# A gated mix of linear attention and a GLU: the gate's transposition, M's loads, the parts of kv and the first forms

## The chip, the cores and the metric

The kernel runs on one core of one Trainium2 chip. The time is that of one execution on the device in microseconds (us), taken as the median of several runs. Beside the runs there is one profiled execution, whose rows are quoted below. The core has five engines that work from queues of their own: TensorE (PE: matrix products into PSUM), VectorE (DVE), ScalarE (ACT), GpSimd (POOL) and SyncE (SP). SyncE and GpSimd issue the transfers here, each in the order of its own queue.

## The reference

x has 2048 rows (tokens) of 640 columns. The result is `g * a + (1 - g) * b` with three parts:

```python
g = _sigmoid((x * gate_w).sum(-1, keepdims=True))

q, k, v = qkv[0], qkv[1], qkv[2]            # 32 heads of 20 columns
phi = lambda t: jnp.where(t > 0, t + 1, jnp.exp(t)) + 1e-6
pq, pk = phi(q), phi(k)
kv = jnp.einsum("bhsd,bhse->bhde", pk, v)
z = jnp.einsum("bhsd->bhd", pk)
num = jnp.einsum("bhqd,bhde->bhqe", pq, kv)
den = jnp.einsum("bhqd,bhd->bhq", pq, z)[..., None] + 1e-6
a = (num / den) @ wo                        # heads side by side

h = _sigmoid(x @ w_gate) * (x @ w_up)       # 1536 columns
b = h @ w_down
```

All inputs are float32. The gate g is one number per token.

## The kernel before

Every product is made in float32r from two halves of each operand: a high half (the operand rounded) and a low half (the operand less its high half). `mm3` (L215 to L218) issues three matmuls, high by high, low by high and high by low. So each operand needs a "form": ScalarE copies the high half, and VectorE subtracts it for the low half (`split`). Most of the larger products are arranged by a scheme of seven products instead of eight (`Block`, steps s1 to s7), with sums of quarters on VectorE. The tile names `ch`, `dd`, `cc` and `rot` are the four kinds of PSUM tile, two buffers each; `tb` holds the sum of b in SBUF.

The order of the instructions on all engines is fixed when the program is built. The class `Order` keeps an estimate of the time of TensorE, ScalarE and VectorE. Work that isn't needed at once is queued with its cost on ScalarE and VectorE, a key and a time from which it is ready; `order.fill()` issues what fits behind TensorE's account, and `order.need(key)` forces what has that key. A few instructions more or less in the account therefore shift the places of others.

The stages, in the profile's time:

- 0 to about 140 us: k = x @ wk and phi(k), and Gt = x' @ phi(k), gathered in `gt`. The columns of `wk` carry the gate's weights too, so that a product's last column is the gate's logit; `vec_copy` puts it into `logit` (one column per tile of 128 tokens, 16 in all). The loop over `k` at the beginning (L747 on) makes forms of the first 128 columns of x and of `wk` as they arrive: `plain_a` (forms `xah`, `xal` of x), `k_plain` (`k1h`, `k1l` and, in the tiles named `pkh` and `pkl`, the second half of `wk`), `plain_b12` (`b12h`, `b12l`).
- about 145 to 190 us: q for half of the tokens (`q_phase(1)`), in 13 steps. In between, `kv_part(hg)` makes kv for six heads at a time from `wv` and `gt` (L1240), takes its diagonal blocks with the mask `bd` (`kvt`) and makes its forms `kvh` and `kvl`; `m_part(hg)` multiplies by that part of `wo` (`woh`, `wol`), copies the product to `ms` and stores it into `m_dram`. M is kv and wo multiplied together, 640x640. With six heads a part there are five parts of 120 columns and one of 40. `order.follow` puts `kvl` behind `kvh`, and `m_part` calls `order.need(("kv", hg))`.
- about 190 to 400 us: `f_phase(1)`, twelve blocks (f = 0 to 11) of the GLU's hidden columns for the second half of the tokens: products with `wg`, `wu` and `ws` (the forms of the gate's, the up's and the summed weights), sigmoid, product, forms `hf`, and the product with `wd`. The forms of weights are also stored, to be read again. In block 1, after step 4, stands `gate_store` (L1113): TensorE multiplies `logit` with an identity matrix in `gs`, which turns 128x16 into 16x128; ScalarE makes sigmoid(l) and sigmoid(-l); SyncE stores both into `gate_dram` and then copies the first, repeated for each head, into `gate_rep`. `gs` is made on VectorE from an iota of GpSimd.
- about 400 to 460 us: q for the first half of the tokens; about 460 to 665 us: `f_phase(0)`, the same twelve blocks for that half. The stored forms are loaded two blocks ahead: in the loop, block f + 2 loads `wg` after step 2, `wu` after step 6 and `ws` after step 7 of block f. In odd blocks from 3 on the products with `wd` are made in pairs by the seven-product scheme (`down_pair`), with a tile `wf` that `load_wf` loads in three pieces. Beside it `queue_m` loads M's rows, makes their forms and stores them into `mp_dram` (key "m", the lowest in rank), and `queue_den` makes the denominators of the attention for a group of 512 tokens: sums on VectorE into `fac`, a store to `den_dram`, four loads that turn it, a reciprocal times the gate, a store to `fac_dram` and four loads back.
- about 665 us to the end: the result's columns from M, phi(q) and the factors, added to b times (1 - g).

For the last stage two kinds of M's pieces are loaded in `f_phase(0)` at block 11 (FC - 1): `load_m(0)` gets forms from `mp_dram`, and `load_ms(0)` and `load_ms(1)` get M's raw columns by `m_rows`: four transfers for each of four column groups, sixteen in all, on GpSimd's queue, into `mt`, `mr` and `mv`. Ahead of them a loop forces what is left with the key "m".

Of the kernel before, what the change touches and what calls it, by code (L numbers as in the profile page):

```python
# [6 lines left out]

F32 = mybir.dt.float32
F32R = mybir.dt.float32r
I32 = mybir.dt.int32  # L10
AF = mybir.ActivationFunctionType
OP = mybir.AluOpType
PSUM = bass.MemoryType.PSUM
# [2 lines left out]
P = 128  # L16
# [7 lines left out]
HW = HALF + 2  # L24
CW = 256
HPG = 6
NHG = -(-H // HPG)
EPS = 1e-6


# [158 lines left out]
def v_cost(w):  # L189
    return 0.155 + w * 0.00104  # L190
# [3 lines left out]
def gated_mix_kernel(ctx: ExitStack, tc: tile.TileContext, xt, xn, wk, wv, wo, wst_q, wst_f, out_t):  # L194
# [17 lines left out]
    def ps_tile(tag):  # L212
        return psum.tile([P, 512], F32, name=tag, tag=tag, bufs=2)
# [47 lines left out]
    bd = common.tile([HPG * DH, HPG, DH], F32, name="bd")  # L261
    zcol = common.tile([P, KC], F32, name="zcol")
    zeps = common.tile([P, 1], F32, name="zeps")
    logit = common.tile([P, S // P], F32, name="logit")
    gs = common.tile([P, P], F32, name="gs")
    fac = common.tile([P, NG, TG], F32, name="fac")
    p_dram = dram.tile([P, KC, NG, TG], F32, name="p_dram")
# [448 lines left out]
    class GTBatch:  # L716
# [18 lines left out]
        def out(self, u):  # L735
# [6 lines left out]
            else:  # L742
                add(dst, ps, dst, "p")


    c0 = chunks[0]
    order.pe = 8.0  # L747
    b0, b1 = KPlain(0), KPlain(1)
    for k in range(KC):
        order.act = max(order.act, order.pe - 1.5)  # L750
        c0.plain_a(k, k + 1)
        k_plain(k)
        if k < 2:
            c0.plain_b12(k, k + 1)
        else:
            c0.plain_b(k, k + 1)
        order.pe = max(order.pe, order.vec)
        b0.k(k)
        if k < 2:
            b1.k(k)  # L760
        if k == 1:
            load_xn(0)
            load_xn(1)
# [10 lines left out]
            split_xn(1)  # L774


    ij = fac[:, 0, :P].bitcast(I32)
    nc.gpsimd.iota(ij, pattern=[[1, P]], base=P, channel_multiplier=-1)
    nc.gpsimd.memset(ones_f, 1.0)
    nc.gpsimd.affine_select(bd, ones_f[:bdn, :bdn].rearrange("p (b c) -> p b c", c=DH),  # L780
                            pattern=[[-DH, HPG], [0, DH]], base=0, channel_multiplier=1,
# [20 lines left out]
    for c in range(1, 4):  # L802
        ck = chunks[c]
        if c == 1:
            a, b = KPlain(2), KPlain(3)
            order.need((ck, "plain"))
            queue_ks()
            queue_xn(2)
            for k in range(KC):
                a.k(k)  # L810
                order.fill()
            a.phi_a()
            for k in range(KC):
                b.k(k)
                order.fill()
                if k == 0:
                    a.phi_b()
                    order.add(0, 0.25, lambda: vec1(gs, ij, float(P), op0=OP.is_equal))
                    queue_qw(2)
            order.need(("ks", 5))  # L820
            for t in range(2):
                k_split(tok(2, t))
        else:
            a, b = KBlock(2 * c), KBlock(2 * c + 1)
            for n in range(1, 6):
                order.need((ck, n))
                if c == 2 and n >= 3:
                    order.need(("ks", (1, 0, 2)[n - 3]))
                getattr(a, f"s{n}")()
                getattr(b, f"s{n}")()  # L830
            order.need((ck, 6))
            if c == 2:
                order.need(("ks", 5))
            if c + 1 < len(chunks):
                chunks[c + 1].load()
            else:
                nx = [Chunk(1, i, None, i * CW, xst_v, (b12h, b12l)) for i in range(2)]
                nx[0].load()
            queue_xn(2 * c)
            a.s6()  # L840
            a.s7()
            a.sum_b()
            a.phi_a()
            b.s6()
            a.phi_b()
            order.need(("pk", 2 * c - 1))
            k_split(tok(2 * c, 0))
            b.s7()
            b.sum_b()
            k_split(tok(2 * c, 1))  # L850
        if c == 3:
            pa_cm.__exit__(None, None, None)
            px_cm = tc.tile_pool(name="px", bufs=1, side="right", reuse_waits="tile")
            px = px_cm.__enter__()
            xf = XForms(px, TG)
            pg_cm = tc.tile_pool(name="pg", bufs=1, side="right", reuse_waits="tile")
            pg = pg_cm.__enter__()
            W, WT = {}, {}

            def wg_tile():  # L860
                return pg.tile([P, 2, D], F32R, name="wg", tag="wg", bufs=2)

            def put(n, i, t):
                WT[n, i] = t
                W[n, i] = [t[:, c] for c in range(2)]

            def store_w(n, i):

                key = n[::2] + (i,)
                w_dram[key] = dram.tile(list(WT[n, i].shape), F32, name="w%s%d%d" % key)  # L870
                nc.gpsimd.dma_start(w_dram[key], f32(WT[n, i]))

            def wg_split(n, src):
                put(n, 0, wg_tile())
                split(*W[n, 0], src)
                if n[0] == "f":
                    order.then(lambda: store_w(n, 0))
            nx[0].f = nx[1].f = xf
        elif c == 1:
            chunks[2].load(lag=6.0)  # L880
        g = GTBatch(c, batches[c])
        order.need(("xn", 2 * c))
        if c < 3:
            chunks[c + 1].queue()
        else:
            queue_xn(7)
        for u in range(4):
            g.part(u, 0, 2, ("rot", "dd", "ch", "cc")[u])
            if u == 0:
                b.phi_a()  # L890
            if u == 1:
                b.phi_b()
        queue_split(2 * c + 1)
        if c < 3:
            queue_xn(2 * c + 1)
        else:
            w_stage = [m1_tile("ma", "w0") for _ in range(2)]
            for n in range(2):
                nc.sync.dma_start(w_stage[n], wst_q[:, n])
            queue_forms(nx)  # L900
        for u in range(2 * KC):
            g.part(u, 2 if u < 4 else 0, 4)
            order.fill()
# [23 lines left out]
    def tt(name, dt=F32, shape=(P, TG)):  # L927
        return pw.tile(list(shape), dt, name=name, tag="t", bufs=4)
# [184 lines left out]
    def gate_store():  # L1113

        n = S // P
        ps = ps_tile("rot")[:n, :P]
        nc.tensor.matmul(ps, logit, gs, start=True, stop=True)
        order.on_pe(4, P)
        t = tt("gates")[:n, :2 * P]
        for i in range(2):  # L1120
            act(t[:, i * P:(i + 1) * P], ps, AF.Sigmoid, "p", scale=1.0 - 2 * i)
        for i in range(2):
            nc.sync.dma_start(gate_dram[i].rearrange("(i p) -> i p", p=P), t[:, i * P:(i + 1) * P])
        nc.sync.dma_start(gate_rep, gate_dram[0].rearrange("(i o p) -> i o p", o=1, p=P).broadcast_to([n, H, P]))

    def queue_den(g, place=None):
# [59 lines left out]
    MV, MO, MO_AT, ZP = {}, {}, {}, []  # L1186

    def hg_slice(hg):
        c0 = hg * bdn
        return c0, min(bdn, D - c0)  # L1190

    def load_mv(hg):
        if hg < NHG:
# [41 lines left out]
    def kv_part(hg, tag="ch"):  # L1235
        c0, w = hg_slice(hg)
        v = MV[hg]
        ps = ps_tile(tag)
        for m in range(KC):
            nc.tensor.matmul(ps[:w, :w], v[:, m, :w], gt[:, m, c0:c0 + w], start=(m == 0), stop=(m == KC - 1))  # L1240
        order.on_pe(10, 2 * bdn)
        kvt = mp.tile([bdn, bdn], F32, name="kvt", tag="kvt", bufs=2)
        vec2(kvt[:w, :w], ps[:w, :w], bd.rearrange("p b c -> p (b c)")[:w, :w], OP.mult, "p")
        kvh = mp.tile([bdn, bdn], F32R, name="kvh", tag="kvh", bufs=3)
        kvl = mp.tile([bdn, bdn], F32R, name="kvl", tag="kvl", bufs=3)
        act(kvh[:w, :w], kvt[:w, :w], AF.Copy, "v")
        KV[hg] = (kvh, kvl)
        order.follow(v_cost(bdn), lambda: vec2(kvl[:w, :w], kvt[:w, :w], f32(kvh[:w, :w]), OP.subtract), ("kv", hg))
        load_mv(hg + 3)

    def m_part(hg, tag="cc"):
        c0, w = hg_slice(hg)
        order.need(("kv", hg))
        order.need(("wo", hg))
        (kvh, kvl), (woh, wol) = KV.pop(hg), WO.pop(hg)
        ms = m1_tile(("ma", "mb")[hg % 2], "ms", F32, bdn)
        for h in range(2):
            ps = ps_tile(tag)
            cs = slice(h * HALF, (h + 1) * HALF)
            mm3(ps[:w, :HALF], kvh[:w, :w], kvl[:w, :w], woh[:w, cs], wol[:w, cs], True, True)  # L1260
            act(ms[:w, cs], ps[:w, :HALF], AF.Copy, "p")
        nc.gpsimd.dma_start(m_dram[c0:c0 + w], ms[:w])
        queue_wo(hg + 2)
# [435 lines left out]
    def f_phase(pr, q, hooks={}):  # L1699
# [51 lines left out]
        for f in range(FC):  # L1751
# [1 line left out]
                order.need(("h", f // 2 - 1, "T3"), False)  # L1753
            down = iter(())
            if not pr and f % 2 and f > 1:
                if f == FC - 1:
                    while any(it[3] == "m" for it in order.spare) or order.pend:
                        order.need("m")
                        order._flush()
                    load_m(0)  # L1760
                    load_ms(0)
                    load_ms(1)
                down = down_pair(f // 2 - 1)
            for s in (3, 4, 5):
                step(f, s)
# [86 lines left out]
    def load_forms(kind, f, *forms):  # L1852
# [1 line left out]
            load_form((kind, 0, f), i)  # L1854

    tail = f_phase(1, q, {
        (1, 4): [gate_store],
        (9, 4): [load_x2],
        (FC - 2, 7): [lambda: load_forms("q", 2, 1, 2)],
        (FC - 1, 2): [lambda: load_forms("q", 2, 0), lambda: queue_a(0, 2), lambda: queue_a(2, 4)],  # L1860
# [402 lines left out]
```

## Time and profile before

| | us |
|---|---|
| runs of before: median (lowest to highest of 3) | 744.03 (742.05 to 745.65) |
| the profiled execution's own time | 745.79 |
| its span, first to last instruction | 744.1 |

The span is the time between the first and the last instruction that the profile shows; what lies around it is the rest of 745.79. In rows of a timeline the columns are: start in us from the span's start, length in us, engine, line, operation, tile written and tiles read, size, count, and in brackets how long the engine had stood idle and what ended that. "SPq" and "POOL DMA_DIRECT2D" rows are issues of transfers; their landing is another row (KB each, us from issue to landing). A matmul's row is longer than its pitch, because matmuls overlap: the distance from start to start is what counts. PEld is the load of the stationary operand.

### The profile page before, as it was taken

How to read it: one execution, taken by the hardware profiler on the slowest of the kernel's cores; microseconds unless marked ns; L12 is line 12 of the kernel's file. 1: busy time of each engine (PE TensorE's matmuls, PEld its weight loads, DVE VectorE, ACT ScalarE, POOL GpSimd, SP SyncE). 2: the span in 40 equal slices, each digit the busy share in tenths (PEclk: the TensorE clock that was granted, in tenths of full speed). 3: DMA queues.
4: the chain of work that ended last, by engine and by line, in shares of the span. 5: the costliest groups of instructions: out<-in, count | busy, mean ns of one | idle time of the engine just before them, and what ended most of it. 6: DMA issues, size and time to landing. Idle time of an engine off the chain costs nothing.

```text
span 744.1 us, 10181 instructions
## 1 busy us (share of the span) xinstructions
PE 736.6 (99%) x3628; PEld 631.4 (85%) x3628; DVE 547.8 (74%) x961; ACT 332.3 (45%) x629; POOL 107.7 (14%) x174
## 2 busy tenths in 40 slices
PE   9999999999999999999999999999999999999998
PEld 7999999987888888888888888888888888788886
DVE  4888676967577778877877964556778777788976
ACT  5664638258555634333434365343323322224541
POOL 0221212012222311312210211000000002200000
PEclk9999999999999999999999999999999999999999
DMA  8564727699888777676966758986869655959312
GB/s 275 121 183 112 197 64 217 177 282 320 295 331 294 264 263 286 220 265 223 370 242 224 297 171 316 359 240 227 278 231 331 253 182 214 274 192 346 116 71 100
DMA packets 69848, 175.23 MB, mean 235 GB/s; under 512 B 11038, under 2 KB 30286, under 8 KB 66213
## 3 DMA queue, kind: packets, MB, share of 16 engines
q1 hardware_dynamic: 52533, 109.46, 45.0%
q0 software_dynamic: 17120, 64.96, 24.8%
q8 instruction: 28, 0.46, 0.3%
q14 instruction: 23, 0.19, 0.1%
q10 hardware_dynamic: 144, 0.16, 0.1%
HBM read 105.65 MB, written 63.91 MB: 228 GB/s over the span
## 4 chain that ended last, share of the span: by engine, by line
PE 88%; DMA 5%; DVE 3%; ACT 2%; SPq 1%; issue 1%; DVEq 0%
PE ch L216 9%; PE ch L217 9%; PE ch L218 9%; PE dd L217 8%; PE dd L216 8%; PE dd L218 8%; PE cc L218 7%; PE cc L216 7%; PE cc L217 7%; PE rot L216 6%; PE rot L217 6%; PE rot L218 6%; DMA xst<-xt 3%; DMA ws<-wf 2%; DMA wo_sb<-wo 1%
## 5 line engine op out<-in xcount | busy, mean ns | idle before, releaser
L228 ACT ACTIVATE c<-ch 128x512 f32<-128x512 f32 x87 | 51.9, 596 | 169.3 <-PE ch L218 167.5
L232 DVE TENSOR_TENSOR hf<-c,hf 128x512 fp32r<-128x512 f32 x63 | 43.3, 689 | 40.4 <-ACT hf L228 40.4
L232 DVE TENSOR_TENSOR c<-cc,c 128x512 f32<-128x512 f32 x54 | 37.2, 689 | 31.9 <-ACT c L228 22.4
L232 DVE TENSOR_TENSOR tb<-dd,tb 128x512 f32<-128x512 f32 x73 | 49.7, 688 | 14.8 <-PE dd L218 14.6
L228 ACT ACTIVATE c<-c 128x512 f32<-128x512 f32 x57 | 35.8, 629 | 49.9 <-DVE c L232 49.6
L228 ACT ACTIVATE hf<-c 128x512 fp32r<-128x512 f32 x63 | 39.2, 624 | 17.4 <-DVE c L232 17.0
L232 DVE TENSOR_TENSOR tb<-rot,tb 128x512 f32<-128x512 f32 (+1 forms) x61 | 40.8, 678 | 6.3 <-PE rot L218 6.1
L216 PE MATMUL ch<-xth,ws 128*128 128x512 f32 x108 | 42.3, 392 | 1.9 <-DMA ws<-wf 1.7
L218 PE MATMUL ch<-xth,ws 128*128 128x512 f32 x108 | 42.0, 389 | 0.0
L217 PE MATMUL ch<-xtl,ws 128*128 128x512 f32 x108 | 42.0, 389 | 0.0
L216 PE MATMUL dd<-xrh,wg 128*128 128x512 f32 x93 | 36.4, 391 | 0.0
L218 PE MATMUL dd<-xrh,wg 128*128 128x512 f32 x93 | 36.2, 389 | 0.0
L217 PE MATMUL dd<-xrl,wg 128*128 128x512 f32 x93 | 36.2, 389 | 0.0
L216 PE MATMUL rot<-pkh,xnh 128*128 128x320 f32 x102 | 31.6, 310 | 0.5 <-DVE gt L232 0.5
L217 PE MATMUL rot<-pkl,xnh 128*128 128x320 f32 x102 | 31.5, 309 | 0.0
L216 PE MATMUL cc<-xbh,ws 128*128 128x512 f32 x81 | 31.5, 389 | 0.0
L217 PE MATMUL cc<-xbl,ws 128*128 128x512 f32 x81 | 31.5, 389 | 0.0
L218 PE MATMUL cc<-xbh,ws 128*128 128x512 f32 x81 | 31.5, 389 | 0.0
L218 PE MATMUL rot<-pkh,xnl 128*128 128x320 f32 x102 | 31.4, 308 | 0.0
L232 DVE TENSOR_TENSOR c<-c,c 128x512 f32<-128x512 f32 x44 | 30.2, 686 | 1.3 <-ACT c L228 0.9
L228 ACT ACTIVATE ws<-wsum 128x512 fp32r<-128x512 f32 (+1 forms) x24 | 16.1, 679 | 22.9 <-DVE wsum L232 22.9
L216 PEld LDWEIGHTS ch<-xth,ws 128*128 128x128 f32 x108 | 20.3, 188 | 6.9 <-issue 2.3
(564 smaller groups left out, 2266.6 us busy)
## 6 DMA issues: line engine op xcount, KB each, us to landing
wf<-ws POOLq DMA_DIRECT2D x12, 1152.0 KB, 6.7
ws<-wf SPq DMA_DIRECT2D x12, 1152.0 KB, 8.4
wst<-wst_f SPq DMA_DIRECT2D x12, 640.0 KB, 4.9
wf<-wg POOLq DMA_DIRECT2D x12, 640.0 KB, 5.2
wd<-wd POOLq DMA_DIRECT2D x12, 640.0 KB, 5.5
wg<-wf SPq DMA_DIRECT2D x12, 640.0 KB, 5.7
xst<-xt SPq DMA_DIRECT2D x10, 640.0 KB, 7.7
wf<-wd SPq DMA_DIRECT2D x10, 640.0 KB, 5.7
```

What stands on the lines that cost most here:

```text
L216: nc.tensor.matmul(out, l_hi, r_hi, start=first, stop=False, skip_group_check=True)
L217: nc.tensor.matmul(out, l_hi, r_lo, start=False, stop=False, skip_group_check=True)
L218: nc.tensor.matmul(out, l_lo, r_hi, start=False, stop=last, skip_group_check=True)
L228: nc.scalar.activation(out, src, fn, **kw)
L232: nc.vector.tensor_tensor(out, a, b, op=op)
```

## The change

Four things are changed.

1. `gate_store` no longer uses TensorE. `logit` gets 32 columns (16 of them zero); ScalarE makes both sigmoids on 128x32; VectorE turns them in blocks of 32x32; SyncE stores them in four transfers (one for each 32 rows) in place of two, and then `gate_rep` as before. The iota, the comparison and `gs`'s identity are gone. The call moves from block 1 to block 2.
2. `load_ms(0)` and `load_ms(1)`, with the loop ahead of them, stand in block 9 (FC - 3) in place of 11; `load_m(0)` stays in 11.
3. kv's heads are cut at 0, 6, 12, 17, 22, 27 and 32: two parts of 120 columns and four of 100. `kvh` is made by VectorE, directly followed by `kvl`; nothing is queued any more.
4. The first pass of the loop at the beginning is written out: VectorE makes `k1h` and `k1l`, ScalarE makes `xah` and the second half's high form.

```diff
-NHG = -(-H // HPG)
+HG = (0, 6, 12, 17, 22, 27, 32)
+NHG = len(HG) - 1
...
-    logit = common.tile([P, S // P], F32, name="logit")
+    logit = common.tile([P, H], F32, name="logit")
...
+    def first_forms():
+
+        x, (xh, xl) = c0.x[0][:, 0:1], c0.f.a_part(0, 1, c0.cs)
+        w1, w3 = wk_st[0][:, lo_h], wk_st[0][:, hi_h]
+        act(xh, x, AF.Copy)
+        vec_copy(k1h[:, 0], w1)
+        vec2(k1l[:, 0], w1, f32(k1h[:, 0]), OP.subtract)
+        vec2(xl, x, f32(xh), OP.subtract, "a")
+        split(k3h[:, 0], k3l[:, 0], w3)
...
-        c0.plain_a(k, k + 1)
-        k_plain(k)
+        if k:
+            c0.plain_a(k, k + 1)
+            k_plain(k)
+        else:
+            first_forms()
...
-    ij = fac[:, 0, :P].bitcast(I32)
-    nc.gpsimd.iota(ij, pattern=[[1, P]], base=P, channel_multiplier=-1)
+    nc.gpsimd.memset(logit[:, S // P:], 0.0)
...
-                    order.add(0, 0.25, lambda: vec1(gs, ij, float(P), op0=OP.is_equal))
...
     def gate_store():
 
         n = S // P
-        ps = ps_tile("rot")[:n, :P]
-        nc.tensor.matmul(ps, logit, gs, start=True, stop=True)
-        order.on_pe(4, P)
-        t = tt("gates")[:n, :2 * P]
+        t = tt("gates").rearrange("p (a n c) -> p a n c", n=2, c=H)
         for i in range(2):
-            act(t[:, i * P:(i + 1) * P], ps, AF.Sigmoid, "p", scale=1.0 - 2 * i)
-        for i in range(2):
-            nc.sync.dma_start(gate_dram[i].rearrange("(i p) -> i p", p=P), t[:, i * P:(i + 1) * P])
+            act(t[:, 0, i], logit, AF.Sigmoid, scale=1.0 - 2 * i)
+        order.on_vec(2 * H, "a")
+        nc.vector.transpose(t[:, 1], t[:, 0])
+        for b in range(P // H):
+            nc.sync.dma_start(gate_dram.rearrange("n (i b c) -> b i n c", b=P // H, c=H)[b],
+                              t[b * H:b * H + n, 1])
...
     def hg_slice(hg):
-        c0 = hg * bdn
-        return c0, min(bdn, D - c0)
+        h0, h1 = HG[hg:hg + 2]
+        return h0 * DH, (h1 - h0) * DH
...
-        act(kvh[:w, :w], kvt[:w, :w], AF.Copy, "v")
+        vec_copy(kvh[:w, :w], kvt[:w, :w])
+        vec2(kvl[:w, :w], kvt[:w, :w], f32(kvh[:w, :w]), OP.subtract)
         KV[hg] = (kvh, kvl)
-        order.follow(v_cost(bdn), lambda: vec2(kvl[:w, :w], kvt[:w, :w], f32(kvh[:w, :w]), OP.subtract), ("kv", hg))
...
-        order.need(("kv", hg))
...
-                if f == FC - 1:
+                if f == FC - 3:
                     while any(it[3] == "m" for it in order.spare) or order.pend:
                         order.need("m")
                         order._flush()
-                    load_m(0)
                     load_ms(0)
                     load_ms(1)
+                elif f == FC - 1:
+                    load_m(0)
...
-        (1, 4): [gate_store],
+        (2, 4): [gate_store],
```

More of the change, by code (lines that the diff above doesn't have):

```diff
@@ L9 @@
 F32R = mybir.dt.float32r
-I32 = mybir.dt.int32
 AF = mybir.ActivationFunctionType
```

## The prediction

> **What bounds the kernel now.** I read first the page's busy shares, then TensorE's waits, since an engine that is busy for almost the whole span can only gain in its waits and in work taken from it.
>
> ```profile
> PE 736.6 (99%) x3628; PEld 631.4 (85%) x3628; DVE 547.8 (74%) x961; ACT 332.3 (45%) x629; POOL 107.7 (14%) x174
> ```
>
> ```profile
> PE ch L216 <- DMA ws<-wf: 1.7, 1, 1.7
> PE rot L216 <- DVE gt L232: 0.5, 1, 0.5
> PE ch L216 <- ACT c L228: 0.2, 1, 0.2
> ```
>
> TensorE is busy for 736.6 of 744.1 us, which leaves 7.5. After the start it waits for others three times (total, times, longest): for a weight transfer, for VectorE and for ScalarE. So this change is worth those waits, as far as it touches them, plus TensorE's own instructions that it removes; everything it does on other engines counts only where it ends or makes such a wait. A matmul of 512 columns follows the one before it after 0.23 us and one of 320 after 0.15 us (the starts in the rows below); what is longer between two starts is the price of a wait.
>
> **M's raw columns (block 9 instead of 11).** The largest wait, by TensorE's timeline:
>
> ```profile
> 638.00 0.39 PE L218 MATMUL cc<-xbh,ws 128*128 128x512 f32 x1
> 640.09 0.47 PE L216 MATMUL ch<-xth,ws 128*128 128x512 f32 x1 [1.70 <-DMA ws<-wf]
> ```
>
> From 638.00 to 640.09 are 2.09 us where 0.23 would do, so the wait costs 1.86. It is step 3 of block 11, which needs that block's `ws`. The queues of SyncE and GpSimd around it, and the times from issue to landing:
>
> ```profile
> 601.71 0.32 SPq L941 DMA_DIRECT2D ws<-wf  x1
> ...
> 626.18 0.33 SPq L941 DMA_DIRECT2D ws<-wf  x1
> ```
>
> ```profile
> 600.30 0.55 POOL L1150 DMA_DIRECT2D den_dram<-fac  x1 [18.48 <-DVE fac L236]
> ...
> 626.89 4.02 POOL L1387 DMA_DIRECT2D mt<-m_dram  x7 [0.20 <-issue]
> ```
>
> ```profile
> ws<-wf SPq DMA_DIRECT2D x1, 1152.0 KB, 11.5
> ...
> ws<-wf SPq DMA_DIRECT2D x1, 1152.0 KB, 8.0
> ...
> ws<-wf SPq DMA_DIRECT2D x1, 1152.0 KB, 13.8
> ```
>
> The three landings are those issued at 516.02, 589.47 and 626.18. The last took 13.8 us; right behind its issue GpSimd sends the sixteen loads of M's columns. The one at 589.47 has the same neighbours on SyncE's queue (three pieces of `wf`, then `wg`, `wu`) and no such loads, and took 8.0. The deadline is 638.23 (638.00 and one step of 0.23), 12.05 us after the issue. By 8.0 it lands with 4 us to spare, by the worst row without these loads, 11.5, with 0.5. I take the whole 1.86 as gained; the other end is 0.
>
> Where the loads go: in the changed kernel's GpSimd stream all sixteen stand behind `den_dram` (600.30) and ahead of the last `fac_dram`. Their source is old by then, and the pieces of M that the new loop would force out stand ahead of block 9 in both programs, so the loop adds no work there. They then meet the `ws` issued at 601.71, which belongs to block 10 and is read from that block's step 3 on, just before the issue at 626.18, some 24 us later: at 13.8 it is still in time. `load_m(0)` stays at block 11.
>
> **The gate turned by VectorE.** TensorE's product goes:
>
> ```profile
> 209.52 0.39 PE L218 MATMUL cc<-xbh,wu 128*128 128x512 f32 x1
> 209.84 0.39 PE L1117 MATMUL rot<-gs,logit 128*16 128x128 f32 x2
> 210.16 0.50 PE L216 MATMUL ch<-xth,ws 128*128 128x512 f32 x1
> 210.49 0.39 PE L217 MATMUL ch<-xtl,ws 128*128 128x512 f32 x1
> ```
>
> 209.52 to 210.49 is 0.97 us, and two steps of 0.23 are 0.45: 0.52 gained. Added are a transposition of 128x64 on VectorE, no row of which exists. With 64 columns it lies between nothing and the subtraction of 128 columns (0.29, row below), to which it is nearer: 0.2. It and two sigmoids of 32 columns move to block 2. VectorE waits there for the sigmoids, with block 2's sums queued behind it and TensorE waiting for their buffers; VectorE is busy for 74% of the span, so I cost this at nothing, and at 0.2 + 0.3 (a ScalarE copy of 120 columns, below) if its slack is gone there. The iota and the comparison that made `gs` fall away, both off TensorE's path.
>
> SyncE issues four gate stores instead of two, and `gate_rep` waits behind them for their landing. Behind those stand `dst` and `wst` loads:
>
> ```profile
> 210.56 1.47 SPq L1123 DMA_DIRECT2D gate_dram<-gates  x2
> 214.25 0.61 SPq L1124 DMA_DIRECT2D gate_rep<-gate_dram  x1
> ...
> 229.90 0.35 SPq L1282 DMA_DIRECT2D dst<-wst_f  x1
> ```
>
> In the changed stream the gate's transfers stand, one block later, right ahead of the `dst` of 229.90, and nothing else is due there. SyncE was held for 3.7 us (210.56 to 214.25) and gets two more issues of some 0.7; if `dst` goes out that much later, it is still loaded for the next pair of blocks. The Trainium skill (DMA: Bandwidth & Descriptors, Specifications) speaks against this store: transfers under 512 B make the engine read, modify and write, and the pieces shrink from 512 B to 128 B. If by it the old hold grew with the number of pieces, fourfold, to some 15 us, `dst` would go out about 9 us late and push forms of the next pair; no product of TensorE reads `dst` itself, so the sum by the rule stays, but it is among what I leave to slower at the end. No run so far shows which holds.
>
> **kv's heads in six parts, kvh by VectorE.** TensorE's time for a part of 120 columns and of 40:
>
> ```profile
> 171.75 1.21 PE L1240 MATMUL ch<-gt,wv_sb 128*120 128x120 f32 x10
> 172.72 0.48 PE L216 MATMUL ch<-xah,wg 128*128 128x512 f32 x1
> ...
> 174.27 0.57 PE L1240 MATMUL rot<-gt,wv_sb 128*40 128x40 f32 x10
> 174.78 0.50 PE L216 MATMUL dd<-xrh,wg 128*128 128x512 f32 x1
> ```
>
> 0.97 and 0.51 us; on the line between them 100 columns take 0.86. Five of the first and one of the second are 5.36, two of the first and four of 0.86 are 5.38: no difference. The products with `wo` keep their 320 columns. What can change is this wait, in TensorE's and ScalarE's order:
>
> ```profile
> 177.68 0.31 PE L218 MATMUL cc<-woh,kvl 120*120 120x320 f32 x1
> 178.23 0.50 PE L216 MATMUL ch<-xth,ws 128*128 128x512 f32 x1 [0.24 <-ACT c L228]
> 178.57 0.39 PE L217 MATMUL ch<-xtl,ws 128*128 128x512 f32 x1
> ```
>
> ```profile
> 177.39 0.30 ACT L228 ACTIVATE kvh<-kvt 120x120 fp32r<-120x120 f32 x1 [2.11 <-DVE kvt L232]
> 177.60 0.58 ACT L228 ACTIVATE c<-ch 128x512 f32<-128x512 f32 x1
> ```
>
> ScalarE stood 2.11 us at `kvh`, waiting for a product of VectorE, and the copy of `ch` that TensorE needs stood behind it. With `kvh` on VectorE that copy no longer has it ahead. 177.68 to 178.57 is 0.89 where 0.15 + 0.23 would do: 0.51 gained, or 0 if VectorE is late instead. VectorE gets six copies, each at most as dear as its 120x120 subtraction (280 ns):
>
> ```profile
> L232 DVE TENSOR_TENSOR kvl<-kvt,kvh 120x120 fp32r<-120x120 f32 x5 | 1.4, 280 | 0.7 <-ACT kvh L228 0.7
> L232 DVE TENSOR_TENSOR qp<-qraw,qp 128x128 fp32r<-128x128 f32 x3 | 0.9, 286 | 0.9 <-ACT qp L228 0.9
> ```
>
> ```profile
> 172.00:182.00 10.00, 9.76 (x59) 7.79 (x58) 8.26 (x19) 7.86 (x18) 3.44 (x7) 1.00 0.90 309
> ```
>
> The last row is a stretch of time: its length, then the busy us (and instructions) of TensorE, its weight loads, VectorE, ScalarE and GpSimd. From 172 to 182 VectorE works 8.26 of 10; three copies make 9.1, and its waits for `kvh` (0.7 in the first row) go. So they fit, without much room.
>
> **First forms by two engines.** The product that decides, and what it waits for:
>
> ```profile
> 6.41 0.41 PE L218 MATMUL cc<-k1h,b12l 128*128 128x322 f32 x1
> ```
>
> ```profile
> 5.47 0.42 ACT L228 ACTIVATE b12h<-xst 128x256 fp32r<-128x256 f32 x1 [0.61 <-DMA xst<-xt]
> ...
> 5.92 0.43 DVE L232 TENSOR_TENSOR b12l<-xst,b12h 128x256 fp32r<-128x256 f32 x1 [0.49 <-ACT b12h L228]
> ```
>
> The first product may start some tenths sooner, but the product at 6.41 needs `b12l`, which ends a chain that a transfer starts at 5.47 and which this edit doesn't touch. VectorE has one copy of 322 columns more to do before 5.92, at most 0.54 (0.43 for 256 columns, scaled), and stands idle there for 0.49. Gain 0; bounds 0.1 either way.
>
> **What moves by itself.** The planner, whose account changed, puts a 128x128 `qp` subtraction ahead of a `gt` sum for which TensorE already waits:
>
> ```profile
> 61.49 0.68 DVE L232 TENSOR_TENSOR xst<-xst 128x512 f32<-128x512 f32 x1
> 62.09 0.48 DVE L232 TENSOR_TENSOR gt<-rot,gt 128x320 f32<-128x320 f32 x1
> ```
>
> Successive sums start 0.08 sooner than their durations say (0.60 for 0.68), so `qp` at 0.286 costs 0.2. Bounds 0 and 0.5 (a second `qp` of 256 columns stands behind it).
>
> **Sum.** -1.86 - 0.52 - 0.51 + 0.2 = -2.69 us, against the profiled execution's 745.79 (span 744.1): 743.1. That execution lies 1.76 above the median of the runs, 744.03; from the median it is **741.3 us**, 0.36% less. What a measurement of this kernel can tell from no change is about 0.5%, or 3.7 us, so I expect a gain that hardly shows.
>
> **Rivals.** (1) `ws` is late all the same, since the pieces of `wf`, `wg` and `wu` ahead of it fill the transfers: for it speaks the row of 11.5, against it the 8.0 with the same neighbours. Only the other terms stay: 743.2.
>
> (2) VectorE becomes late between 172 and 182, and TensorE waits there for `kvl`, `wol` or a freed buffer: the 0.51 goes, and up to 6 x 0.28 = 1.7 is added: 741.8 to 743.5. For it: the 8.26 of 10; against it: the waits for ScalarE that vanish.
>
> (3) The other side. The sixteen loads now run while the denominators of group 1 are being turned. SyncE waits for `den_dram`, then issues four loads of `fac`, and VectorE's queue holds the sum that reads them:
>
> ```profile
> den_dram<-fac POOLq DMA_DIRECT2D x1, 256.0 KB, 4.3
> ...
> fac<-den_dram SPq DMA_DIRECT2D x4, 64.0 KB, 5.6
> ```
>
> ```profile
> 623.27 0.74 DVE L232 TENSOR_TENSOR fac<-fac 128x256 f32<-128x256 f32 x2
> ```
>
> Now that is 600.30 + 4.3, about 2 of issues, 5.6: near 612, 11 us early. If both transfers took the 13.8 that `ws` took beside these loads, it were 630: 6.6 us late, with block 10's sums held behind it, and the time 741.3 + 6.6 = 747.9. It is slower than now once the chain lasts 25.7 us (22.97 to 623.27, and the 2.69 of gain). Against it: `den_dram` is issued ahead of the loads.
>
> (4) The wait for `gt` ends too, since the transfer that made VectorE late there comes sooner: the 0.2 isn't paid and the 0.5 of the waits' row is gained: 740.6.
>
> **How the numbers follow.** Forecast 0.55, (1) 0.18, (2) 0.13, (3) 0.07, (4) 0.07. Forecast's own spread is that of the runs shown, 742.05 to 745.65, about 1.8 to either side. Range 739.7 to 744.2: it holds (1), (2) and (4) and leaves out (3) and the low end of the forecast's spread. Faster by over 0.5% is under 740.3: a quarter of the forecast and a third of (4): 0.16. Slower by over 0.5% is over 747.7: the worst end of (3), and what I don't foresee, the rule on small transfers included: 0.05. The rest is 0.79.
>
> **What would show it.** In the changed profile: TensorE's waits without `ws<-wf` and without ScalarE's `c`; the landing of the `ws` issued near 624 at 8 to 11 us; GpSimd's loads of M between 601 and 618; no L1117 product; the wait for `gt` near 62 at 0.7 to 0.8; the product with `b12l` at 6.4. I am wrong if the wait for `ws` stays, if TensorE waits for VectorE between 154 and 186, or if VectorE's sum of `fac` waits for a transfer.

## The result, and the profile after

| | median us (lowest to highest, runs) |
|---|---|
| before | 743.92 (742.05 to 745.65, 10) |
| after | 745.9 (745.01 to 746.75, 10) |
| after / before | 1.0025, 95% interval 1.0015 to 1.0036 |

The changed kernel is 2.0 us slower, where a gain of 2.7 was forecast: 745.9 lies above the range of 739.7 to 744.2, and the sign is the other one. The profiled execution of after took 745.01 with a span of 743.3, which is the shortest of its ten. The first lines of its page:

```profile
span 743.3 us, 10191 instructions
...
PE 738.5 (99%) x3626; PEld 632.4 (85%) x3626; DVE 550.8 (74%) x968; ACT 330.5 (44%) x622; POOL 107.7 (14%) x174
```

TensorE has two matmuls fewer, and is busy 1.9 us longer. The whole of its waits, in the view that counts them:

```profile
PE rot L304 <- DVE warm L301: 1.3, 1, 1.3
```

Only the start is left. The waits for `ws`, `gt` and `c` are gone. TensorE's timeline of after, at the places which the prediction showed of before:

```profile
6.19 0.35 PE L218 MATMUL cc<-k1h,b12l 128*128 128x322 f32 x1
...
62.05 0.31 PE L218 MATMUL rot<-pkh,xnl 128*128 128x320 f32 x1
62.20 0.30 PE L216 MATMUL rot<-pkh,xnh 128*128 128x320 f32 x1
...
176.84 0.31 PE L218 MATMUL cc<-woh,kvl 100*100 100x320 f32 x1
176.98 0.40 PE L216 MATMUL ch<-xth,ws 128*128 128x512 f32 x1
...
637.45 0.39 PE L218 MATMUL cc<-xbh,ws 128*128 128x512 f32 x1
637.67 0.39 PE L216 MATMUL ch<-xth,ws 128*128 128x512 f32 x1
```

Start to start is 0.15, 0.14 and 0.22 us at the three pairs; before, it was 0.55 near 178 (177.68 to 178.23) and 2.09 at 638. Every wait that was to go went. SyncE's and GpSimd's issues and VectorE's work behind that, each from its engine's timeline of after:

```profile
221.09 3.20 SPq L1133 DMA_DIRECT2D gate_dram<-gates  x4
227.41 0.61 SPq L1135 DMA_DIRECT2D gate_rep<-gate_dram  x1
228.12 0.56 SPq L1292 DMA_DIRECT2D dst<-wst_f  x1
...
603.55 3.31 SPq L1167 DMA_DIRECT2D fac<-den_dram  x4
625.63 0.33 SPq L952 DMA_DIRECT2D ws<-wf  x1
```

```profile
600.72 4.60 POOL L1397 DMA_DIRECT2D mt<-m_dram  x8 [0.73 <-issue]
...
613.94 2.27 POOL L1397 DMA_DIRECT2D mv<-m_dram  x4
```

```profile
61.49 0.28 DVE L232 TENSOR_TENSOR qp<-qraw,qp 128x128 fp32r<-128x128 f32 x1
61.96 0.49 DVE L232 TENSOR_TENSOR gt<-rot,gt 128x320 f32<-128x320 f32 x1 [0.19 <-PE rot L218]
...
220.83 0.24 DVE L1131 STREAM_TRANSPOSE gates<-gates 128x64 f32<-128x64 f32 x1
...
622.70 0.74 DVE L232 TENSOR_TENSOR fac<-fac 128x256 f32<-128x256 f32 x2
```

M's loads go out between 600.72 and 616. VectorE's sum of `fac` waits for no transfer. So where did the time go? Not into a wait. A table by stretches shows it: two kernels, the same stages, TensorE busy without a pause in both. Of before:

```profile
250.00:400.00 150.00, 150.00 (x663) 124.21 (x662) 117.74 (x216) 61.59 (x118) 32.98 (x53) 1.00 0.76 275
490.00:610.00 120.00, 120.00 (x531) 99.38 (x530) 84.96 (x134) 39.95 (x70) 4.31 (x8) 1.00 0.75 257
655.00:730.00 75.00, 75.00 (x333) 62.10 (x332) 66.06 (x112) 31.75 (x58) 0.00 (x0) 1.00 0.50 182
```

Of after:

```profile
250.00:400.00 150.00, 150.00 (x661) 123.98 (x661) 116.67 (x213) 59.30 (x114) 31.02 (x50) 1.00 0.73 268
490.00:610.00 120.00, 120.00 (x527) 98.59 (x526) 84.74 (x133) 39.58 (x69) 9.48 (x17) 1.00 0.74 255
655.00:730.00 75.00, 75.00 (x326) 61.03 (x325) 64.96 (x109) 31.67 (x58) 0.00 (x0) 1.00 0.51 185
```

The second number with its count is TensorE, the 1.00 its granted clock. In the same time after gets through 2, 4 and 7 matmuls less, which is 13 x 0.227 = 3.0 us in these three stretches. Summed over all starts behind 190 us, the products of 512 columns take 3.4 us more than in before. Many of them are a little slower. The view of groups by shape gives the shortest, median and longest row of a group in ns. Of before, then of after:

```profile
L216 PE MATMUL dd<-hf,wf x50: 389/389/389, 492.7 to 657.2; 128*128 128x512 f32 x50
...
L216 PE MATMUL dd<-pq,wf x15: 389/389/389, 679.6 to 718.4; 128*128 128x512 f32 x15
```

```profile
L216 PE MATMUL dd<-hf,wf x50: 389/394/399, 491.0 to 654.9; 128*128 128x512 f32 x50
...
L216 PE MATMUL dd<-pq,wf x15: 393/394/399, 677.6 to 717.4; 128*128 128x512 f32 x15
```

In before all are alike to the nanosecond, and start to start is 226.7 ns. In after a part of them takes up to 10 ns longer. A mean per group (389 against 390 on the page) hides this; the spread shows it.

### The profile page after: what moved, and what is told of

It reads as the page before. It is cut to its first block, busy times and chain, and to the rows that moved or that the text cites. A ratio compares the mean times of both kernels' runs of the same rounds, so it can differ in the third digit from the quotient of the medians.

```text
span 743.3 us, 10191 instructions
## 1 busy us (share of the span) xinstructions
PE 738.5 (99%) x3626; PEld 632.4 (85%) x3626; DVE 550.8 (74%) x968; ACT 330.5 (44%) x622; POOL 107.7 (14%) x174
## 4 chain that ended last, share of the span: by engine, by line
PE 96%; DVE 1%; ACT 1%; DMA 1%; issue 0%; SPq 0%; DVEq 0%
PE ch L216 10%; PE ch L217 10%; PE ch L218 10%; PE dd L218 8%; PE dd L216 8%; PE dd L217 8%; PE cc L216 7%; PE cc L218 7%; PE cc L217 7%; PE rot L216 7%; PE rot L218 6%; PE rot L217 6%; DMA xst<-xt 1%; DVE xst L232 0%; PE rot L304 0%; ACT xth L228 0%
```

## The experiments

### Which part of the change makes the products slower

The change makes `logit` 32 columns wide, 64 B more per partition, and `logit` lies near the bottom of SBUF. In the built program everything that is stacked on it moves up by 64 B; what is stacked down from the top stays. Start addresses, modulo 256 B:

```
tiles                                          before   after
gs, fac, tb, hf (7 of 8), wd, wf, dst, ds       224      32
ws, wg, wu, pq, pt, c, x forms, hf (1 of 8)     224     224
```

(The tiles of the GLU and of the last stage; in the first 140 us some forms lie at other offsets in both kernels.) Four kernels tried the addresses, with the order of every engine's instructions left alone. e1:

```diff
-    logit = common.tile([P, H], F32, name="logit")
+    common.tile([P, S // P], F32, name="gap")
     gs = common.tile([P, P], F32, name="gs")
+    logit = gs[:, :H]
```

> The changed kernel with one thing undone: the logits lie in the first 32 columns of gs, so that every tile is at the address it has in the kernel before (the old 64 B of logit stay empty). Theory A (addresses): the 64 B by which logit grew put hf, wf, wd, tb and their neighbours at another offset than ws, wg, pq and the x forms, and TensorE's products of 512 columns follow one another in about 228.7 to 231 ns in place of 226.7. Then this kernel has 226.7 throughout, saves the 3.5 us which the products of 512 columns after 190 us have lost in the changed kernel, and takes 745.9 - 3.5 = 742.4 us, 0.2% under the kernel before. Theory B (traffic: the moved transfers and VectorE's added work disturb TensorE's reads): the pitch stays as it is in the changed kernel and the time is 745.9.

742.54 us (742.11 to 743.44); beside the runs of before that were made with it, 744.52, the ratio is 0.9976, interval 0.9967 to 0.9986. e2, in the kernel before:

```diff
-    logit = common.tile([P, S // P], F32, name="logit")
+    logit = common.tile([P, H], F32, name="logit")[:, :S // P]
```

> The kernel before, with a logit tile of 32 columns of which 16 are used: the order of every engine is untouched, and all tiles behind logit lie 64 B higher. A: the pitch of the products of 512 columns grows to 227.3 between 230 and 420 us, to 228.7 between 490 and 620 and to 231 behind 650, as in the changed kernel, and the time is 743.9 + 3.5 = 747.4. B: no change, 743.9.

747.36 us, ratio 1.0053 (1.0034 to 1.0072). So theory A holds in both directions, by amounts that were written down: moving addresses alone costs the kernel before 3 us, and moving them back makes the changed kernel the faster of the two. Theory B is out: in e2 nothing but addresses differs. The last stage in both, e1 first:

```profile
655.00:730.00 75.00, 75.00 (x332) 62.12 (x331) 66.26 (x111) 32.23 (x59) 0.00 (x0) 1.00 0.53 189
```

```profile
655.00:730.00 75.00, 75.00 (x326) 60.92 (x325) 64.70 (x109) 31.05 (x57) 0.00 (x0) 1.00 0.50 182
```

332 like before (333), 326 like after. e3 is the changed kernel with 48 columns in `logit`, e4 the same with 80:

```diff
-    logit = common.tile([P, H], F32, name="logit")
+    logit = common.tile([P, 48], F32, name="logit")[:, :H]
```

> The changed kernel with a logit tile of 48 columns: the tiles behind it lie 128 B above their places in the kernel before, at 96 modulo 256 where ws, wg, pq and the x forms are at 224. A with a period of 128 B: as good as the old addresses, 742.4. A with a period of 256 B: slow like the changed kernel, 745.9, or in other places. B: 745.9.

> The changed kernel with a logit tile of 80 columns: the tiles behind it lie 256 B above their places in the kernel before, again at 224 modulo 256. A with a period of 128 or 256 B: 742.4 and a pitch of 226.7. If the pitch here is as slow as in the changed kernel, it is not the offset modulo 256 that decides, but the place itself; B: 745.9.

e3: 745.36, ratio 1.0011 (0.9997 to 1.0025). e4: 742.13, ratio 0.9969 (0.9956 to 0.9981). 256 B further is as good as the old place, 128 B is not: of the distances tried, only 256 restores it. The last stage in e3 and in e4:

```profile
655.00:730.00 75.00, 75.00 (x325) 60.88 (x324) 64.83 (x109) 31.66 (x58) 0.00 (x0) 1.00 0.49 182
```

```profile
655.00:730.00 75.00, 75.00 (x333) 62.12 (x332) 66.25 (x112) 32.35 (x59) 0.00 (x0) 1.00 0.52 189
```

Is 32 a poor place, or are two places poor? e5 adds a gap at the top to e2:

```diff
+    top = ctx.enter_context(tc.tile_pool(name="top", bufs=1, side="right"))
+    top.tile([P, 48], F32, name="gap")
     pa_cm = tc.tile_pool(name="pa", bufs=1, side="right")
```

> The kernel of e2 (the kernel before, tiles behind logit 64 B higher), and at the other end of SBUF a gap of 192 B, so that the tiles there (ws, wg, pq, the x forms of both halves) stand at 32 modulo 256 too. A1 (what costs is that two groups of tiles stand at different offsets): the pitch of the products of 512 columns is 226.7 ns again and the time that of the kernel before, 744.5. A2 (32 modulo 256 is a poor offset by itself): every product after 190 us is slow, at 229 to 233 ns, and the time is above e2's 747.4, up to 744.5 + 2390 x 0.004 = 754.

743.5, ratio 0.9994 (0.9979 to 1.001): A1. With all tiles at 32 the loss is gone, as the last stage shows:

```profile
655.00:730.00 75.00, 75.00 (x332) 62.13 (x331) 66.04 (x112) 32.37 (x59) 0.00 (x0) 1.00 0.51 187
```

What matters is that the tiles agree. But which, and with whom? In e2, products whose operands both lay at 224 were slow too, mostly while VectorE added into `tb`. e6 moves `tb` alone, modulo 256 (what is stacked on it lies a whole 256 B higher):

```diff
+        down_pool[0].tile([P, 16], F32, name="gap0")
         tb = down_pool[0].tile([P, KC, 2, TG], F32, name="tb")
+        down_pool[0].tile([P, 48], F32, name="gap1")
```

> The kernel before with only tb moved to 32 modulo 256 (64 B ahead of it and 192 B behind it, so that all that follows is 256 B higher, at 224 modulo 256 as before). No product reads or writes tb; VectorE adds into it. A3 (an engine whose tile stands at another offset slows TensorE's reads too): the products of 512 columns that run while VectorE adds into tb take about 3 ns more, as in e2 (229.7 beside tb<-dd,tb with both operands at 224); with 134 sums of 0.68 us that is 91 us or 400 products, 1.2 us in all: 745.7. A4 (only TensorE's own operands count): 226.7 throughout and 744.5.

744.25, ratio 1.0005 (0.9992 to 1.0018), and

```profile
655.00:730.00 75.00, 75.00 (x333) 62.10 (x332) 66.03 (x112) 32.01 (x59) 0.00 (x0) 1.00 0.51 185
```

A4: VectorE's tile does not count, and the coincidence with `tb` in e2 was no cause. e11 moves, of TensorE's operands, only the stationary `wd` and `wf` (and with them the tiles that they are made from, which TensorE doesn't read):

```diff
         down_pool.append(down_cms[0].__enter__())
+        down_pool[1].tile([P, 16], F32, name="gap0")
...
-        return down_pool[1].tile([P, 2, WF], F32R, name="wf", tag="wf")
+        t = down_pool[1].tile([P, 2, WF], F32R, name="wf", tag="wf")
+        if "gap" not in turn:
+            turn["gap"] = down_pool[1].tile([P, 48], F32, name="gap3")
+        return t
...
+        down_pool[1].tile([P, 16], F32, name="gap2")
         turn.update(c=4, h=0)
```

> The kernel before with only wd, wf and the tiles that they are made from at 32 modulo 256 (gaps of 64 B ahead and 192 B behind); hf, pq, pt, ws, wg and the x forms stay at 224. 784 products of 512 columns then have a stationary operand at another offset than their moving one. W (the two operands of one product must agree): these go to 233.5 ns, as pq<-wf did in e2, from 226.7: 784 x 6.8 = 5.3 us, 749.5, more than e2. N (what counts is that neighbouring products differ): slow too, but in the order of e2, 747.4, with the products next to a change of operands. If the stationary operand's offset doesn't count at all: 744.2 and 226.7.

750.53, ratio 1.0081 (1.0065 to 1.0097): six us for 64 B, where W gave five and N three. Before, then e11:

```profile
L216 PE MATMUL dd<-hf,wd x60: 389/389/389, 223.9 to 417.7; 128*128 128x512 f32 x60
```

```profile
L216 PE MATMUL dd<-hf,wd x60: 393/398/398, 225.6 to 422.0; 128*128 128x512 f32 x60
...
L216 PE MATMUL dd<-hf,wf x50: 393/396/398, 497.1 to 663.6; 128*128 128x512 f32 x50
```

Here not one product with `wd` escapes. Its weight loads did not get longer:

```profile
L216 PEld LDWEIGHTS dd<-hf,wf x50: 187/188/188, 496.9 to 663.3; 128*128 128x128 f32 x50
```

So in the rows it is the matmuls that got longer, not the loads of the stationary operand; the ends of matmuls in a profile are modelled, so which of the two reads is held up is not shown. The starts of each trace, grouped by the offsets of the product's operands (the next product's stationary operand at the same offset), give the mean distance to the next start:

```
moving / stationary, modulo 256      e2              e3 (96 for 32)   e11
224 / 32                             233.5 ns x163   233.0 x163       233.5 x736
32 / 224                             229.5 x68       233.0 x68        none
32 / 32                              228.8 x573      227.1 x573       none
224 / 224                            227.3 x1484     227.0 x1488      227.5 x1556
before, all 224 / 224                226.7 x2383
```

A product whose two operands lie at different offsets costs 3 to 7 ns more, of 227. In the trace of after that is the smaller part of the loss: 1.4 us in 250 such products. The other 2.1 us fall on products whose operands agree, and all of it on the first ten behind a change from one pair of offsets to another (678 products); from the eleventh on they follow one another at 226.7 again (1453 products).

e11 shows this most plainly. Behind the last product with `wd` or `wf`, six products at 224 / 224 take 230.7, 230.9, 235.5, 228.3, 231.3 and 230.2 ns (means over 35 to 47 changes), and then 226.7. In its trace these cost 1.2 us, beside 5.1 in the products with unlike operands. So W holds, and N has a part in it.

Why the loss trails, these runs don't tell. Nor do they tell whether it is a product's own stationary operand that counts, or the next one's, which is loaded while the product runs (its PEld row begins about 3 ns behind the product's row). Where a group that agrees at one offset meets a group that agrees at the other (61 changes), the last product ahead of the change is followed after 226.3 ns in e2 and after 232.6 in e3.

The products of 320 columns in the first 140 us have tiles at all sorts of offsets, in both kernels, and show no such loss: 146.6 ns in before, 146.7 in after.

### What the four parts are worth without it

e7 has one part in the kernel before, M's raw columns in block 9:

```diff
-                if f == FC - 1:
+                if f == FC - 3:
...
-                    load_m(0)
                     load_ms(0)
                     load_ms(1)
+                elif f == FC - 1:
+                    load_m(0)
```

> The kernel before with one part of the change alone: M's raw columns loaded in block 9. The prediction's step: the wait for ws at step 3 of block 11 goes and with it 1.86 us: 744.5 - 1.9 = 742.6. Rival: 1.86 was the wait of one slow execution (745.79, and the profile of e2 shows 0.28 at the same place), and an ordinary execution has a shorter one, 0.3 to 1: 743.5 to 744.2.

743.72, ratio 0.9999 (0.9984 to 1.0015): the rival. Its profile has no wait at 638, but one in an earlier block, long before M's loads:

```profile
528.86 0.39 PE L218 MATMUL cc<-xbh,ws 128*128 128x512 f32 x1
529.72 0.47 PE L216 MATMUL ch<-xth,ws 128*128 128x512 f32 x1 [0.48 <-DMA ws<-wf]
```

e8 is e1 with kv's parts and `kvh` as before:

```diff
-        vec_copy(kvh[:w, :w], kvt[:w, :w])
-        vec2(kvl[:w, :w], kvt[:w, :w], f32(kvh[:w, :w]), OP.subtract)
+        act(kvh[:w, :w], kvt[:w, :w], AF.Copy, "v")
+        order.follow(v_cost(bdn), lambda: vec2(kvl[:w, :w], kvt[:w, :w], f32(kvh[:w, :w]), OP.subtract), ("kv", hg))
```

It asks about a wait that e1 has and before has not, and what ScalarE does ahead of it (waits, then ScalarE's timeline, of e1):

```profile
PE cc L216 <- ACT ms L228: 0.6, 1, 0.6
```

```profile
169.35 0.58 ACT L228 ACTIVATE qe<-dd 128x512 f32<-128x512 f32 x1
169.82 0.59 ACT L228 ACTIVATE qr<-dd 128x512 f32<-128x512 f32 x1
170.30 0.77 ACT L228 ACTIVATE ms<-cc 120x320 f32<-120x320 f32 x2
```

> The kernel of e1 (the changed kernel at the old addresses) with the kv part undone: parts of six heads, kvh by ScalarE again. If the new wait of 0.55 us for ScalarE's ms near 170 us comes from the kv part, it goes, and the wait for ScalarE's c near 178 (0.5) comes back: 742.5 - 0.7 + 0.5 = 742.3, no difference that the times can tell, but another row among TensorE's waits. If it comes from the transfer of xst that ends ScalarE's idle time ahead of it, it stays beside the wait for c: 743.0.

742.82, ratio 0.9977 (0.9962 to 0.9992), and neither expectation: this execution has no wait but the start's. e9 is the gate's part alone, e10 the gate and block 9, e12 the first forms alone; their edits are those of the change, with `logit` in `gs` as in e1 where the gate is changed.

> The kernel before with the gate part alone (logits in the first columns of gs, so all tiles stay where they were). The prediction's step: TensorE's product for the gate goes, 0.52 us, nothing else moves on TensorE: 744.2 - 0.5 = 743.7, with the waits for ws, for gt near 62 and for c near 178 as they come in an execution of the kernel before. Rival: the four stores and the transposition make TensorE wait in block 2 or 3, near 218 to 236 us: 744.2 or more.

> The kernel of e9 with M's raw columns loaded in block 9 as well; it differs from e8 only in the first forms, which are those of the kernel before. Prediction: 743.7 - 1.9 = 741.8, and as fast as e8 (742.8), since the first forms cost and bring nothing. Rival: the early part of the kernel decides more than thought: with the old first forms TensorE still waits for gt near 62 us in many executions (0.7 to 0.9, as in the profiles of the kernel before and of e7, but in none of the five profiles that have the new first forms); then it takes 743.3 or more and spreads like the kernel before, over 3 us and more.

> The kernel before with the first forms alone. The prediction's step: nothing gained or lost, 744.2 to 744.5, with the spread of the kernel before (3 us and more between the fastest and the slowest of a dozen executions). Theory F, from e8 (742.8, 2.4 us from the fastest to the slowest) beside e10 (744.0, 3.4 us): the first forms start TensorE 0.1 to 0.4 us sooner and thereby shift the transfers of xt, so that slow executions with a wait for gt near 62 us become rare; then the fastest executions stay where they are (742 to 742.5), the slow ones go, and the median is 743.0 to 743.4.

e9: 744.45, ratio 0.9992 (0.9977 to 1.0008), the time of its rival, but its profile has no wait in blocks 2 and 3. e10: 744.04, ratio 0.9993 (0.9981 to 1.0005). e12: 744.06 (742.82 to 748.19), ratio 0.9999 (0.998 to 1.0018): theory F falls, the first forms alone neither move the median nor narrow the spread. e10 has the time of its rival, but its profile has no wait for `gt`, so what keeps it 1.2 us behind e8 isn't shown. No single part can be told from nothing. e9's waits have the one for `ms` too, without kv's new parts, so these don't make it:

```profile
PE cc L215 <- ACT ms L227: 0.9, 1, 0.9
PE ch L215 <- ACT c L227: 0.4, 1, 0.4
```

and e12 has the wait for `ws` near its old place:

```profile
637.22 0.39 PE L218 MATMUL cc<-xbh,ws 128*128 128x512 f32 x1
638.78 0.47 PE L216 MATMUL ch<-xth,ws 128*128 128x512 f32 x1 [1.17 <-DMA ws<-wf]
```

Fourteen profiles of one order or nearly one order, side by side, say more than one. The excess of start to start over the usual pitch, in us (a dash: under 0.2):

```
profile     gt, 62   ms, 170   c, 178   ws, 638
before       0.70      -        0.40     1.86
e2            -        -        0.42     0.28
e5            -        -        0.41      -
e6            -        -        0.32     0.49
e7           0.88      -        0.56      -   (0.64 at 529)
e9            -       1.06      0.56      -
e10           -       0.34      0.56      -
e11          1.42     0.63      0.56     1.59
e12           -        -         -       1.33
e8            -        -         -        -
after         -       0.24       -        -
e1            -       0.72       -        -
e3            -       1.07       -        -
e4            -       0.97       -        -
```

## Why the prediction was wrong

**The step that failed** stands in the prediction's first part: "So this change is worth those waits, as far as it touches them, plus TensorE's own instructions that it removes". That takes the pitch of the products that stay ("A matmul of 512 columns follows the one before it after 0.23 us") as given, and the sum has no term for what the change does to it. "Gate turned by VectorE" was costed as work (a product, a transposition, stores), while its one line in the memory's layout, `logit` from 16 to 32 columns, was not costed at all. It is worth +3.4 us, more than all other terms together. e1 and e2 show the cause; e5 and e11 show that it is unlike offsets of TensorE's operands that cost, in the products that have them and in those right behind.

**The wait for `ws`, -1.86**, had the right mechanism and the wrong size. It went, as the trace of after shows, and at 638 none of the seven profiles with the loads in block 9 has it. But 1.86 was one execution's price, in the only profile there was, itself 1.8 us above the median. In the seven profiles with the loads in block 11 it is 1.86, 0.28, 0, 0.49, 0, 1.59 and 1.33, mean 0.79; with the loads in block 9 the one of 0.64 at 529 makes a mean of 0.09. So 0.7 is nearer. Subtracting a whole outlier from a median was the error.

**The gate's product, -0.52**: right in the traces, though e9's times can't show it. Between the same products on either side of it, after gains 0.52. The transposition took 0.24 us (0.2 estimated), and no product waited for it. SyncE was held for 6.3 us (221.09 to 227.41) where it was 3.7. The Trainium skill's rule on small transfers (DMA: Bandwidth & Descriptors, Specifications) had been read as up to 15 us; the measured hold is less than half of that, and 3.2 of it are the four issues. `dst` went out at 228.12 (229.90 before), and nothing waited for it.

**The wait for `c`, -0.51**: it is in eight of the ten profiles with kv's old part (mean of the ten 0.38) and in none of the four with the new one. But in those four TensorE waits for `ms` at 170 instead, 0.24 to 1.07, mean 0.75, against a mean of 0.20 in the ten. The wait for `ms` was in no rival: ScalarE's copies `qe` and `qr` stand ahead of it. That kv's new parts make this wait isn't shown (e9 has it without them); on these means the part wins nothing (-0.38 + 0.55), and with e8 as fast as e1 the times agree. VectorE was not late (rival 2).

**The `qp` ahead of the `gt` sum, +0.2**: the order came as forecast (61.49), but the wait beside it was gone, since the `xt` transfer landed sooner (ScalarE's `xbh`, which it releases, began at 57.47 instead of 59.73): the `gt` sum waited for TensorE (0.19), not the other way. That is rival 4. In the table the wait comes in 3 of the 8 profiles without the new first forms, mean 0.38, and in none of 6 with them; e12's times say that this isn't a saving which can be counted on.

**The first forms, 0**: right, as far as e12 can tell.

**Rival 3** did not come: `fac<-den_dram` went out at 603.55 and VectorE's sum ran at 622.70 without a wait.

Put together from these means: -0.70 (`ws`) - 0.52 (gate) + 0.17 (kv) - 0.38 (`gt`) = -1.4 us, and with 3.4 more for the pitch +2.0. The medians differ by 745.9 - 743.92 = +2.0. And e1, where only the pitch is put right, measured -2.0 against the runs beside it, with an interval of -2.5 to -1.0. That the parts add up like this is bookkeeping over a few profiles each; shown by runs of their own are only the pitch and the sum of the rest.

Both e1 and e4 beat the kernel before, by 0.2 to 0.3%. What was left of the change's worth, the layout had taken and more.

## What to carry to other kernels

Where one tile's size changes, compare all start addresses of the built program before and after: in a stage full of products of 512 columns, all of TensorE's operands should keep one offset modulo 256 B, and a gap of a few columns restores it. Where an engine is busy for 99% of the span, look at the distance from start to start in a stage, not only at waits, since a loss of 2% there is invisible in busy shares. A wait's price read from a single profile is one draw: size it from several executions, or bound it from zero.

## What was not expected of the hardware

- The effect of the offset itself: 3 to 7 ns in 227 for a product of 512 columns, without a trace among the waits, at a granted clock of 1.00, and going on for some products behind a change. The Trainium skill (TensorE: Matmul & The Clock Gate, step 1 of "Step-by-step: what each phase is for") says that TensorE reads the moving and the stationary operand through two independent ports, so that loading the next weights takes nothing from the running product. e11 shows that the two operands are not without effect on each other: where only the stationary ones were moved, 736 products went from 226.7 to 233.5 ns in the mean. Whether that is the loads taking from the running product, which the Trainium skill rules out, no run shows.
- How long TensorE runs slowly at the start differs between executions. In e10's profile the products of 322 columns are still 0.27 us apart behind 8 us, in before they are 0.15 apart there:

```profile
8.39 0.47 PE L215 MATMUL ch<-k1h,xah 128*128 128x322 f32 x1
8.66 0.47 PE L216 MATMUL ch<-k1l,xah 128*128 128x322 f32 x1
```

  Its hundredth product starts 2.3 us later than that of before, though no wait of that size stands there. The clock column prints 1.00 for both, but in the first microseconds it has nothing to go by: the trace's record of the clock begins at 10.66 us in e10 and at 5.17 in before, and close to these times the products fall from 0.27 or 0.28 to 0.15. The same page of the Trainium skill (Part 1, on the clock gate) says that the window which releases the clock runs freely, so that the number of slow products changes from run to run; this trace agrees. The 2.3 us are of the order of the spread of 3 to 6 us among executions of one kernel, against which no single part of this change could be measured; how much of that spread it makes isn't shown.
